# Column-tiled token values and a re-ordered second softmax half in a segment-recurrent attention kernel

## The chip, the cores and the metric

The kernel runs on one core of a Trainium2 chip. The metric is the device time of one execution in microseconds. The kernel before was run three times: 953.64, 951.12 and 949.33 us, median 951.12. The profile is one further execution.

The engines are named as in the profile: PE is TensorE (PEld its weight loads, which overlap the matmuls), DVE is VectorE, ACT is ScalarE, POOL is GpSimd, SP is SyncE, which issues DMAs here.

## The reference

A layer with two blocks on 2048 tokens of width 640: a recurrent attention over 64 segments, and a feed-forward block.

```python
def _A_ref(x, mem0, Wq, Wk, Wv, Wo, seg_len):      # seg_len 32, M 8, H 32, Dh 128
    mem = mem0
    for s in range(n_seg):                          # 64 segments, one after the other
        h = jnp.concatenate([mem, xs], axis=1)      # 8 memory rows + 32 tokens
        q = jnp.einsum('btd,dhe->bhte', h, Wq)
        k = jnp.einsum('btd,dhe->bhte', h, Wk)
        v = jnp.einsum('btd,dhe->bhte', h, Wv)
        scores = jnp.where(mask, q @ k.T * scale, -1e9)
        p = _softmax(scores, axis=-1)
        o = jnp.einsum('bhqk,bhke->bhqe', p, v)
        o = jnp.einsum('bhte,hed->btd', o, Wo)
        mem = o[:, :M, :]                           # goes into the next segment
        outs.append(o[:, M:, :])

h  = x + _A_ref(_layernorm(x), ...)
h2 = h + _B_ref(_layernorm(h), ...)                 # relu(h @ w1 + b1)**2 @ w2 + b2
```

The memory rows of one segment are the attention's output of the segment before. That makes the 64 segments a chain.

## The kernel before, in words

`step(b, sp)` handles segment `s = 4 * b + sp`. It projects q, k and v of 32 rows: the 8 memory rows and the first 24 tokens. The last 8 tokens of each segment (the "tails") don't depend on the memory; their projections and output rounds are cut into units (`tail_units`, `wo_tail_units`) that a planner (`portion`) hands out, some 8 a step. They stand in the list `fill` and are issued on PE where it would wait.

`manual_schedule` means that each engine does its instructions in the order in which the code issues them. Nothing is moved by a scheduler. The order inside one step is:

1. `run_late`: flips (DVE transposes) of tail rows that are due, then `owed.pop()()`, the `turns` of the step before (L692 to L701): two DVE transposes that bring the token weights `pkt` and `pk` into the form that the token values need (`pTt`, `pTk`), and two POOL products `pTx`.
2. Projections q0, k0, q1, k1 (L234): 5 chunks of the depth, each with 4 matmuls of 32 weight columns by 512 moving columns that lie side by side in four column groups of the array. ACT evicts, DVE flips (L258, L488), POOL spreads the memory rows' q into `qz` (L443, L445).
3. The softmax of the memory rows, in two halves of 16 heads: `scores(n)` (L498), `soft1(n)`: max on DVE (L504) and exponential on ACT (L507), `soft2(n)`: reciprocal, a product with `same` (L514) and the weighting (L518 for half 0, L521 for half 1), and the turn into a block layout `pB`: for half 0 in `soft3` (DVE transpose L529, then four copies of one 32-partition block each, L532: one on DVE, one on ACT, two on POOL), for half 1 by L521 and the transpose L524. Between these, PE does the projection of v (L234, tiles px) and the token scores (L590). ACT evicts v in two halves (L597, L611).
4. `values(0)`, `values(1)` (L540, L545): the memory rows' outputs, column-tiled. `values_out(n)` evicts them into `oT`, half 0 on ACT (L246), half 1 on DVE (L244). Ahead of and behind `values(0)` stand fill units. Between the halves PE does two rounds of the output projection (`wo_rounds`, L270), behind `values(1)` the other 14. One round is 16 heads' worth split by `head`: 4 matmuls of 320 columns. Rounds 0 to 7 need only half 0 of `oT`, rounds 8 to 15 need half 1.
5. The token softmax on DVE and ACT (L615, L648, L650, L655, L657).
6. `wo_out`: ACT and DVE fold the output (L285 to L287) and DVE transposes it into the next step's `hT` (L382), in two parts. This is the chain to the next segment. POOL weighs the tokens in between (`weigh`, L664, L666).
7. The rest of `fill`, then `token_values(s - 1)` (L423, L428): the tokens' outputs of the segment before, 32 + 8 matmuls with 32-row weights by 128 columns and 32 moving columns, four row groups side by side, into four PSUM banks. `token_out` evicts them on ACT (L434), POOL copies the tails' part (L436).

PSUM tiles `po0` and `po1` have two banks each. `hnT0` is a buffer for the feed-forward block; some tail rows are parked in it early, and the feed-forward fills it from step 59 on.

```python
        if last:
            turns()
        else:
            owed.append(turns)
```

Of the kernel before, what the change touches and what calls it, by code (L numbers as in the profile page):

```python
# [9 lines left out]
ALU = mybir.AluOpType  # L10
AX = mybir.AxisListType
F32 = mybir.dt.float32
BF16 = mybir.dt.bfloat16
# [3 lines left out]
def kernel(  # L17
# [16 lines left out]
    nc = tc.nc  # L34
# [3 lines left out]
    SEG = 32  # L38
# [203 lines left out]
    def evac(dve, out_, in_):  # L242
        if dve:
            nc.vector.tensor_copy(out=out_, in_=in_)  # L244
        else:
            nc.scalar.copy(out=out_, in_=in_)  # L246
# [169 lines left out]
    def token_values(s, v, vt4, po):  # L416

        sp = s % 4
        pTk, pTx = back.pop()
        for i in range(HG):  # L420
            for g in range(G):
                r = slice(32 * g, 32 * g + 32)
                nc.tensor.matmul(po[0][g][:, i * 32:(i + 1) * 32], lhsT=v[r, i * E:(i + 1) * E], rhs=pTk[r, i, :],  # L423
                                 start=(i == 0), stop=False, skip_group_check=True)
        for u in range(2):
            for g in range(G):
                r = slice(32 * g, 32 * g + 32)
                nc.tensor.matmul(po[0][g][:, u * 128:(u + 1) * 128].rearrange("p (j q) -> p j q", q=32)[:, :, 0:TL],  # L428
                                 lhsT=vt4[r, sp, u, :], rhs=pTx[r, u], start=False, stop=True, skip_group_check=True)

    def token_out(s, po):
        for h in range(2):
            gs = slice(2 * h, 2 * h + 2)
            nc.scalar.copy(out=oTg[:, gs, :, :, 0:SEG],  # L434
                           in_=po[1][h][:, :, 0:256].rearrange("p g (n j q) -> p g n j q", n=2, q=32))
        nc.gpsimd.tensor_copy(out=oTts[s // 4 % 2][:, :, s % 4 * TL:(s % 4 + 1) * TL], in_=oT[:, :, 0:TL])  # L436
# [7 lines left out]
            else:  # L444
                nc.gpsimd.tensor_copy(out=d, in_=src[:, :, 3, :])  # L445

    prevs, spent, owed = [], [0], []

    def end_output(s):
        pw = chn.tile([128, 512], F32, tag="ch", name="pw")  # L450
# [3 lines left out]
    def step(b, sp, v=None):  # L454
# [5 lines left out]
            v = s2.tile([128, EG], BF16, tag="v", name="v")  # L460
        if not ready:
            run_late(s, 1.6 - spent.pop())
            owed.pop()()
        if sp == 1 and b + 1 < NB:
            tails_v_in(b + 1, nc.sync)

# [26 lines left out]
        def scores(n):  # L493
            sm = chn.tile([128, 512], F32, tag="ch", name="sm")
            for j in range(4):
                for g in range(G):
                    p = n * 16 + g * 4 + j
                    nc.tensor.matmul(sm[32 * g:32 * g + 32, 0:NK], lhsT=qz[:, p, :], rhs=kT[:, p, :],  # L498
                                     start=(j == 0), stop=(j == 3), skip_group_check=True)
            sms[n] = sm  # L500

        def soft1(n):
            mx = s2.tile([128, 1], F32, tag="mx", name="mx")
            nc.vector.tensor_reduce(out=mx[:], in_=sms[n][:, 0:NK], op=ALU.max, axis=AX.X, negate=True)  # L504
            em = s2.tile([128, SEG + NK], BF16, tag="em", name="em", bufs=1)
            zm = s2.tile([128, 1], F32, tag="zm", name="zm")
            nc.scalar.activation(out=em[:, SEG:], in_=sms[n][:, 0:NK], func=ACT.Exp, bias=mx[:, 0:1], scale=1.0,  # L507
                                 accum_out=zm[:])
            ems[n], zms[n] = em, zm

        def soft2(n):
            rm = s2.tile([128, 1], F32, tag="rm", name="rm")
            nc.vector.reciprocal(out=rm[:], in_=zms[n][:])
            nc.vector.tensor_tensor(out=ems[n][:, 0:SEG].rearrange("p (j k) -> p j k", k=TL),  # L514
                                    in0=ems[n][:, 2 * SEG:].unsqueeze(1).to_broadcast([128, 4, TL]), in1=same[:], op=ALU.mult)
            if n == 0:
                pm = s1.tile([128, HG, TL], BF16, tag="pkt", name="pm")[:].rearrange("p i k -> p (i k)")
                nc.vector.tensor_scalar(out=pm, in0=ems[n][:, 0:2 * SEG], scalar1=rm[:, 0:1], scalar2=None, op0=ALU.mult)  # L518
                return pm
            pm = s1.tile([128, HG, 32], BF16, tag="pk", name="pm")[:].rearrange("p (g a) k -> p g (a k)", g=G)  # L520
            nc.vector.scalar_tensor_tensor(out=pm, in0=ems[n][:, 0:2 * SEG].unsqueeze(1).to_broadcast([128, G, 2 * SEG]),  # L521
                                           scalar=rm[:, 0:1], in1=own[:].unsqueeze(2).to_broadcast([128, G, 2 * SEG]),
                                           op0=ALU.mult, op1=ALU.mult)
            nc.vector.transpose(out=pBs[1][:], in_=pm)  # L524
            return pBs[1]

        def soft3(pm):
            pT = s1.tile([128, 2, 32], BF16, tag="pTt", name="pT")[:].rearrange("p u k -> p (u k)")
            nc.vector.transpose(out=pT, in_=pm)  # L529
            for g, copy in enumerate((nc.vector.tensor_copy, nc.scalar.copy, nc.gpsimd.tensor_copy, nc.gpsimd.tensor_copy)):  # L530
                r = slice(32 * g, 32 * g + 32)
                copy(out=pBs[0][r, g], in_=pT[r])  # L532
            return pBs[0]

        def values(n, pB, po):
            cols = po[:, 0, 0:128]
# [9 lines left out]
                                 start=False, stop=True, skip_group_check=True)  # L546

        def values_out(n, po):
            evac(n == 1, oT[:, n * 16:(n + 1) * 16, SEG:NK], po[:, 0, 0:128].rearrange("p (a m) -> p a m", m=M))

        project("q", wq, qT, 0)
        if not last and not ready:
# [46 lines left out]
            proj(wv, "half", lhs, 1, ps1, 0, 1)  # L599
        if not last:  # L600
            pm0 = soft2(0)
            scores(1)
            soft1(1)
            pT0 = soft3(pm0)
        if not ready:
            proj(wv, "half", lhs, 1, ps1, 1, 2)
        token_scores(1)
        if not ready:
            proj(wv, "half", lhs, 1, ps1, 2, DC)
        if not ready:  # L610
            nc.scalar.copy(out=v[:, 512:1024], in_=ps1[:])  # L611
        if not last:
            pT1 = soft2(1)
        def causal(skv):
# [9 lines left out]
        if last:  # L624
            run(fill, max(1, (len(fill) - 3) // 2), held, True)
            token_values(s - 1, *prevs[-2], po)
            token_out(s - 1, po)
            settle(held, True)
            run(fill, 2, held)
            settle(held, True)  # L630
            causal(skv)
        else:
            ahead = 0 if ready else (len(fill) + 1) // 2
            left = len(fill) - ahead
            run(fill, ahead // 2, held, True)
            values(0, pT0, po[1][0])
            values_out(0, po[1][0])
            run(fill, len(fill) - left, held)
            pw = chn.tile([128, 512], F32, tag="ch", name="pw")
            if not ready:  # L640
                wo_rounds(lambda p: oT[:, p, M:NK], pw, range(2))
            values(1, pT1, po[1][1])
            causal(skv)
            values_out(1, po[1][1])
            settle(held, True)
# [23 lines left out]
        if not last:  # L669
            if ready:  # L670
                for k in range(4):
                    run(fill, SEG0[k])
                    wo_rounds(lambda p: oT[:, p, M:NK], pw, [2 * k + h for h in (0, 1, 8, 9)])
            else:
                wo_rounds(lambda p: oT[:, p, M:NK], pw, range(2, 16))
            o = wo_out(pw, ((s + 1) // 4, (s + 1) % 4), weigh)
            if s > 1:
                store_main(o, s - 2)
            held = []
            run(fill, 100, held)  # L680
            if s:
                token_values(s - 1, *prevs[-2], po)
                token_out(s - 1, po)
            settle(held, True)
            for _, f in held:
                late.append((0.35, f, s + 1))
            tails_in((s + 1) // 4, (s + 1) % 4)
        else:
            weigh()
        spent.append(0.5 * min(len(mid), 2))  # L690
        run(mid, 2)
        def turns():  # L692
            pTt = s1.tile([128, 2, 32], BF16, tag="pTt", name="pTt")
            nc.vector.transpose(out=pTt[:], in_=pkt[:].rearrange("p (u j) k -> p u (j k)", u=2))
            pTx = s1.tile([128, 2, 4, TL], BF16, tag="pTx", name="pTx")
            for u in range(2):
                nc.gpsimd.tensor_tensor(out=pTx[:, u], in0=pTt[:, u, 0:TL].unsqueeze(1).to_broadcast([128, 4, TL]),
                                        in1=same[:], op=ALU.mult)
            pTk = s1.tile([128, HG, 32], BF16, tag="pTk", name="pTk")
            nc.vector.transpose(out=pTk[:], in_=pk[:])  # L700
            back.append((pTk, pTx))  # L701
        if last:
            turns()
        else:
            owed.append(turns)

    NT = 512
    NK4 = NT // 128
# [35 lines left out]
    f1T = ck(FC * NT).rearrange("p (c t) -> p c t", c=FC)  # L744
    hnT0 = const.tile([128, DC, NT], BF16, name="hnT0")
    ht0 = [const.tile([128, D], BF16, name="ht0%d" % k) for k in range(NK4)]
    halves = lambda t: [(t[:, 0:512], False), (t[:, 512:1024], False)]
    parked = halves(s2.tile([128, EG], BF16, tag="v", name="parkv"))
    parked += halves(oTts[0][:].rearrange("p h r -> p (h r)"))
# [337 lines left out]
```

## Time and profile before

| What | Value |
|---|---|
| Median of three runs | 951.12 us (949.33 to 953.64) |
| The profiled execution | 947.79 us, span 945.8 us |
| PE busy | 919.7 us (97%) |
| DVE busy | 696.5 us (74%) |
| ACT busy | 553.4 us (59%) |
| POOL busy | 311.6 us (33%) |
| One step in the middle of the loop | 11.7 to 12.2 us |
| Granted TensorE clock | 0.998 |

A line of the trace in order of time reads: start in us from the span's start, duration in us, engine, line of the kernel, operation, output tile, inputs, shapes, count, and in brackets the idle time before it and what ended it. Instructions of one kind that follow each other are merged into one row. Matmul ends are modelled, so starts are the safer numbers: the distance between the starts of two groups is what the first one cost.

A group's row in the list of waits counts a weight load's idle time in full, also where the matmuls before it were still streaming.

### The profile page before, as it was taken

Reading aid. Unit: us, or ns where it says so; the run is one execution under the profiler, and the core shown is the slowest. Engines: PE = TensorE matmul, PEld = TensorE weight load, DVE = VectorE, ACT = ScalarE, POOL = GpSimd, SP = SyncE. Lnnn points to the kernel's source line nnn. Section 1 sums busy time; section 2 is a strip of 40 time slices with the busy share of each in tenths; the row PEclk is TensorE's granted clock in tenths of the full one; section 3 lists DMA queues with packets and bytes.
Section 4 is the critical chain, followed back from the end, with each engine's and each line's share of the span. In section 5 each row is a group of like instructions: output and inputs, shape, how many; then the busy total and the mean of one; then the engine's idle time right before and its main releaser. Section 6 shows DMA issues by size and latency. Waiting matters only on the chain.

```text
span 945.8 us, 55978 instructions
## 1 busy us (share of the span) xinstructions
PE 919.7 (97%) x24749; PEld 537.0 (57%) x24760; DVE 696.5 (74%) x2131; ACT 553.4 (59%) x1460; POOL 311.6 (33%) x1002
## 2 busy tenths in 40 slices
PE   5979999999999999999999999999999999999998
PEld 2435555555555565555555656566556555565555
DVE  5168888778877887777878787878887888556632
ACT  2546666666666666666666666666666666523321
POOL 2123333333333333333333333333333333343300
PEclk9999999999999999999999999999999999999999
DMA  9983201010101000100111010101010221734320
GB/s 352 405 270 70 41 19 29 14 30 14 23 20 28 18 20 25 21 25 9 37 22 24 11 30 14 32 15 31 8 33 7 54 43 21 221 93 92 91 57 28
DMA packets 65875, 56.66 MB, mean 60 GB/s; under 512 B 37384, under 2 KB 61712, under 8 KB 63712
## 3 DMA queue, kind: packets, MB, share of 16 engines
q1 hardware_dynamic: 65392, 52.74, 20.1%
q8 instruction: 194, 3.18, 1.5%
q14 instruction: 49, 0.40, 0.2%
q0 software_dynamic: 224, 0.33, 0.1%
q10 hardware_dynamic: 16, 0.01, 0.0%
HBM read 38.37 MB, written 9.44 MB: 51 GB/s over the span
## 4 chain that ended last, share of the span: by engine, by line
PE 90%; DMA 4%; DVE 2%; SPq 2%; ACT 1%; issue 1%; POOL 0%; ACTq 0%; DVEq 0%
PE ps L234 23%; PE px L234 21%; PE pw L270 16%; PE pk L234 7%; PE y L1044 6%; PE ps L992 6%; PE ps L270 3%; DMA wq<-in_A_Wq_dram 2%; PE po L423 2%; SPq L151 2%; PE po L540 1%; PE sm L498 1%; PE ps L590 1%; DMA wo<-in_A_Wo_dram 1%; PE po L545 1%
## 5 line engine op out<-in xcount | busy, mean ns | idle before, releaser
L234 PEld LDWEIGHTS <-hT 128*32 128x32 bf16 x7680 | 182.1, 96 | 158.7 <-DVE hT L382 22.1
L270 PE MATMUL pw<-wo,oT 128*32 128x320 bf16 x4224 | 168.7, 299 | 3.5 <-DMA wo<-in_A_Wo_dram 1.2
L234 PE MATMUL px<-wv,hT 128*32 128x512 bf16 x2520 | 166.5, 377 | 0.0
L270 PEld LDWEIGHTS <-oT 128*32 128x32 bf16 x4224 | 110.4, 96 | 45.8 <-ACT oT L246 20.7
L258 DVE STREAM_TRANSPOSE qT<-row 128x512 bf16<-128x512 bf16 x128 | 89.0, 696 | 24.9 <-ACT row L253 24.3
L664 POOL TENSOR_TENSOR pkt<-ek,rk 128x64 bf16<-128x64 bf16 x64 | 18.9, 295 | 254.5 <-ACT otmp L286 248.5
L655 ACT ACTIVATE ek<-tk 128x320 bf16<-128x320 f32 x64 | 30.1, 471 | 106.1 <-DVE tk L650 106.1
L234 PE MATMUL ps<-wq,hT 128*32 128x512 bf16 x1260 | 81.5, 383 | 3.2 <-DVE hT L382 2.8
L234 PE MATMUL ps<-wk,hT 128*32 128x512 bf16 x1280 | 80.3, 379 | 0.0
L234 PE MATMUL px<-wq,hT 128*32 128x512 bf16 x1260 | 79.2, 379 | 0.0
L234 PE MATMUL pk<-wk,hT 128*32 128x512 bf16 x1240 | 78.0, 379 | 0.0
L1000 ACT ACTIVATE wv<-ps,b1f 128x512 bf16<-128x512 f32 (+1 forms) x56 | 37.6, 672 | 66.6 <-PE ps L992 66.1
L434 ACT CAST oT<-po 128x512 bf16<-128x512 f32 x128 | 68.7, 589 | 10.2 <-PE po L428 5.6
L234 PEld LDWEIGHTS <-hTt 128*32 128x32 bf16 x1920 | 53.3, 97 | 35.2 <-issue 3.3
L443 POOL COPY qz<-qT 128x96 bf16<-128x96 bf16 x126 | 33.5, 266 | 86.0 <-DVE qT L258 85.7
L1044 PE MATMUL y<-wq,wk 128*128 128x320 bf16 x416 | 58.9, 299 | 0.2
L485 ACT CAST row<-ps 128x256 bf16<-128x256 f32 x126 | 40.8, 375 | 30.0 <-PE ps L234 29.1
L253 ACT ACTIVATE row<-ps 128x512 bf16<-128x512 f32 x93 | 54.7, 611 | 5.2 <-PE ps L234 4.3
L253 ACT ACTIVATE row<-px 128x512 bf16<-128x512 f32 x63 | 37.6, 597 | 32.2 <-PE px L234 30.6
L498 PEld LDWEIGHTS <-qz 128*32 128x32 bf16 x2016 | 37.6, 95 | 25.8 <-issue 2.0
L532 POOL COPY pB<-pT 32x64 bf16<-32x64 bf16 x126 | 29.4, 233 | 66.0 <-DVE pT L529 63.4
L285 ACT COPY otmp<-pw 64x96 f32<-64x96 f32 (+2 forms) x129 | 28.9, 224 | 37.9 <-DVE o L287 20.4
(137 smaller groups left out, 1854.7 us busy)
## 6 DMA issues: line engine op xcount, KB each, us to landing
wv<-in_A_Wv_dram SPq DMA_DIRECT2D x5, 1024.0 KB
wq<-in_A_Wq_dram SPq DMA_DIRECT2D x5, 1024.0 KB
wk<-in_A_Wk_dram SPq DMA_DIRECT2D x5, 1024.0 KB
wo<-in_A_Wo_dram SPq DMA_DIRECT2D x8, 640.0 KB
o_all<-o SPq DMA_DIRECT2D x256, 7.5 KB
vt<-vt_d SPq DMA_DIRECT2D x60, 64.0 KB
xt<-in_A_x_dram SPq DMA_DIRECT2D x19, 160.0 KB
wq<-in_B_w_dram SPq DMA_DIRECT2D x1, 2080.0 KB
```

Of the source, the lines that this page charges most:

```text
L234: nc.tensor.matmul(ps[32 * k:32 * k + 32, :], lhsT=lhs(c), rhs=wr[:, c, n, k], start=(c == 0), stop=(c == DC - 1))
L253: nc.scalar.mul(out=row, in_=ps, mul=scale)
L258: nc.vector.transpose(out=dst[:, n * 16:(n + 1) * 16, 0:32], in_=row.rearrange("p (h e) -> p h e", e=32))
L270: nc.tensor.matmul(pw[32 * j:32 * j + 32, c0:c0 + DH], lhsT=lhs(p), rhs=wov2[:, head(p), ch], start=(h == 0), stop=(h == 15))
L434: nc.scalar.copy(out=oTg[:, gs, :, :, 0:SEG], in_=po[1][h][:, :, 0:256].rearrange("p g (n j q) -> p g n j q", n=2, q=32))
L443: nc.gpsimd.tensor_copy(out=d.rearrange("p a (j f) -> p a j f", j=3)[:, :, :, 0:M], in_=src[:, :, 0:3, :])
L485: nc.scalar.copy(out=row[:, u * 256:(u + 1) * 256], in_=ps[:, u * 256:(u + 1) * 256])
L498: nc.tensor.matmul(sm[32 * g:32 * g + 32, 0:NK], lhsT=qz[:, p, :], rhs=kT[:, p, :], start=(j == 0), stop=(j == 3), skip_group_check=True)
L655: nc.scalar.activation(out=ek[:], in_=tk[:], func=ACT.Exp, scale=1.0)
L992: nc.tensor.matmul(ps[:], lhsT=w1[:, c, fc * 128:(fc + 1) * 128], rhs=hnT[:, c, :], start=(c == 0), stop=(c == DC - 1))
L1000: nc.scalar.activation(out=r[:, 0:w], in_=ps[:, 0:w], func=ACT.Relu, bias=b1f[:, fc:fc + 1], scale=1.0)
L1044: nc.tensor.matmul(y[hh][:, 0:DH], lhsT=f1T[:, fc, k * 128:(k + 1) * 128], rhs=w2[:, fc, cs], start=(fc == 0 and not hf), stop=(fc == FFUL ...
```

## The change

Five things are done.

- In steps 5 to 57 (`wide`) the token values are column-tiled: the token weights are laid out as block diagonals, `pBk` (128 x 8 x 128) by four POOL copies of a 32-partition block a step, and `pBx` (128 x 2 x 128) by two POOL products, which replace the two for `pTx`. Both lie in `hnT0`. The weights of the matmul are 32 columns of all 128 rows of `v`, and 128 columns move; the outputs lie in one bank each of `po0` and `po1`. In step 5 POOL clears `pBk` and makes a mask `both`. The copies are issued by `diagonal(s - 1)` in step s, behind `soft1(1)`.
- `soft3` of the first half (its transpose and the ACT and POOL copies) is issued ahead of `scores(1)` and the second max; the DVE copy comes behind that max.
- The second half of v is evicted in two copies of 256 columns, one ahead of `values_out(0)` and one behind it. `values_out(1)` goes from DVE to ACT.
- Four output rounds instead of two stand ahead of `values(1)`.
- `turns` is no longer owed to the next step's start; its instructions are issued at the end of the step, ahead of `run_late`.

```diff
@@ token_values
         pTk, pTx = back.pop()
+        if wide(s):
+            for n in range(2):
+                for j in range(4):
+                    for k in range(4):
+                        nc.tensor.matmul(po[1][n][32 * k:32 * k + 32, 1, j * 128:(j + 1) * 128],
+                                         lhsT=v[:, (n * 4 + j) * E + 32 * k:(n * 4 + j) * E + 32 * k + 32],
+                                         rhs=pBk[:, n * 4 + j], start=(j == 0), stop=False, skip_group_check=True)
+                for k in range(4):
+                    nc.tensor.matmul(po[1][n][32 * k:32 * k + 32, 1, :].rearrange("p (a q) -> p a q", q=32)[:, :, 0:TL],
+                                     lhsT=vt4[:, sp, n, 32 * k:32 * k + 32], rhs=pBx[:, n],
+                                     start=False, stop=True, skip_group_check=True)
+            return
...
+    def wide(s):
+        return 5 <= s <= NS - 7
+
+    def diagonal(s):
+        if s == 4:
+            nc.gpsimd.memset(pBk, 0.0)
+            for g in range(G):
+                nc.gpsimd.tensor_tensor(out=both[:, :, g], in0=same[:],
+                                        in1=own[:, g:g + 1].unsqueeze(2).to_broadcast([128, 4, TL]), op=ALU.mult)
+        if wide(s):
+            pTk = back[-1][0]
+            for g in range(G):
+                r = slice(32 * g, 32 * g + 32)
+                nc.gpsimd.tensor_copy(out=pBk[r, :, 32 * g:32 * g + 32], in_=pTk[r])
+
     def token_out(s, po):
         for h in range(2):
+            if wide(s):
+                nc.scalar.copy(out=oT[:, h * 16:(h + 1) * 16, 0:SEG].rearrange("p (g j) q -> p j g q", j=4),
+                               in_=po[1][h][:, 1, :].rearrange("p (j g q) -> p j g q", j=4, g=G))
+                continue
...
         if not ready:
             run_late(s, 1.6 - spent.pop())
-            owed.pop()()
...
-        def soft1(n):
+        def soft1(n, then=None):
             mx = s2.tile([128, 1], F32, tag="mx", name="mx")
             nc.vector.tensor_reduce(out=mx[:], in_=sms[n][:, 0:NK], op=ALU.max, axis=AX.X, negate=True)
+            if then:
+                then()
...
-            for g, copy in enumerate((nc.vector.tensor_copy, nc.scalar.copy, nc.gpsimd.tensor_copy, nc.gpsimd.tensor_copy)):
+            def part(g):
                 r = slice(32 * g, 32 * g + 32)
-                copy(out=pBs[0][r, g], in_=pT[r])
-            return pBs[0]
+                (nc.vector.tensor_copy, nc.scalar.copy, nc.gpsimd.tensor_copy, nc.gpsimd.tensor_copy)[g](out=pBs[0][r, g], in_=pT[r])
+            for g in range(1, G):
+                part(g)
+            return pBs[0], lambda: part(0)
...
-            evac(n == 1, oT[:, n * 16:(n + 1) * 16, SEG:NK], po[:, 0, 0:128].rearrange("p (a m) -> p a m", m=M))
+            evac(False, oT[:, n * 16:(n + 1) * 16, SEG:NK], po[:, 0, 0:128].rearrange("p (a m) -> p a m", m=M))
...
             pm0 = soft2(0)
+            pT0, then = soft3(pm0)
             scores(1)
-            soft1(1)
-            pT0 = soft3(pm0)
+            soft1(1, then)
+        if s and not last:
+            diagonal(s - 1)
...
-            nc.scalar.copy(out=v[:, 512:1024], in_=ps1[:])
+            nc.scalar.copy(out=v[:, 512:768], in_=ps1[:, 0:256])
+            if last:
+                nc.scalar.copy(out=v[:, 768:1024], in_=ps1[:, 256:512])
...
             values_out(0, po[1][0])
+            if not ready:
+                nc.scalar.copy(out=v[:, 768:1024], in_=ps1[:, 256:512])
...
-                wo_rounds(lambda p: oT[:, p, M:NK], pw, range(2))
+                wo_rounds(lambda p: oT[:, p, M:NK], pw, range(4))
...
-                wo_rounds(lambda p: oT[:, p, M:NK], pw, range(2, 16))
+                wo_rounds(lambda p: oT[:, p, M:NK], pw, range(4, 16))
...
-        def turns():
-            pTt = s1.tile([128, 2, 32], BF16, tag="pTt", name="pTt")
...
-        if last:
-            turns()
-        else:
-            owed.append(turns)
+        pTt = s1.tile([128, 2, 32], BF16, tag="pTt", name="pTt")
+        nc.vector.transpose(out=pTt[:], in_=pkt[:].rearrange("p (u j) k -> p u (j k)", u=2))
+        pTx = s1.tile([128, 2, 4, TL], BF16, tag="pTx", name="pTx")
+        for u in range(2):
+            if wide(s):
+                nc.gpsimd.tensor_tensor(out=pBx[:, u].rearrange("p (a q) -> p a q", q=TL),
+                                        in0=pTt[:, u, 0:TL].unsqueeze(1).to_broadcast([128, 16, TL]),
+                                        in1=both[:].rearrange("p j g q -> p (j g) q"), op=ALU.mult)
+                continue
+            nc.gpsimd.tensor_tensor(out=pTx[:, u], in0=pTt[:, u, 0:TL].unsqueeze(1).to_broadcast([128, 4, TL]),
+                                    in1=same[:], op=ALU.mult)
+        pTk = s1.tile([128, HG, 32], BF16, tag="pTk", name="pTk")
+        nc.vector.transpose(out=pTk[:], in_=pk[:])
+        back.append((pTk, pTx))
...
+    hn0 = hnT0[:].rearrange("p c t -> p (c t)")
+    pBk = hn0[:, 0:1024].rearrange("p (i a) -> p i a", a=128)
+    pBx = hn0[:, 1024:1280].rearrange("p (u a) -> p u a", a=128)
+    both = hn0[:, 1280:1408].rearrange("p (j g q) -> p j g q", j=4, g=G)
```

More of the change, by code (lines that the diff above doesn't have):

```diff
@@ L445, in spread @@
                 nc.gpsimd.tensor_copy(out=d, in_=src[:, :, 3, :])
-    prevs, spent, owed = [], [0], []
+    prevs, spent = [], [0]
     def end_output(s):
@@ L691, in step @@
         run(mid, 2)
-        def turns():
-            pTt = s1.tile([128, 2, 32], BF16, tag="pTt", name="pTt")
[L694 to L701, printed above, removed]
-        if last:
-            turns()
-        else:
-            owed.append(turns)
+        pTt = s1.tile([128, 2, 32], BF16, tag="pTt", name="pTt")
[12 more added lines that the diff above has]
+        back.append((pTk, pTx))
     NT = 512
```

## The prediction

> **What bounds the kernel now.** I read the page's busy line first, then the trace in order of time, in two places: the seam between two segment steps (408 to 412 us) and the middle of a step (414 to 418 us). The page:
>
> ```profile
> PE 919.7 (97%) x24749; PEld 537.0 (57%) x24760; DVE 696.5 (74%) x2131; ACT 553.4 (59%) x1460; POOL 311.6 (33%) x1002
> ```
>
> PE is busy for 97% of the span, but its ends are modelled. So I use starts. The seam:
>
> ```profile
> 408.21 0.39 PE L234 MATMUL ps<-wv,hTt 128*32 128x512 bf16 x4
> 408.53 0.27 PEld L423 LDWEIGHTS <-v 32*128 32x128 bf16 x32 [0.42 <-issue]
> 408.53 0.37 PE L423 MATMUL po<-pTk,v 32*128 32x32 bf16 x32
> 408.59 0.28 DVE L382 STREAM_TRANSPOSE hT<-o 128x96 bf16<-128x96 bf16 x1
> 408.75 0.24 PE L428 MATMUL po<-pTx,vt 32*128 32x32 bf16 x8
> 408.92 1.30 PE L234 MATMUL ps<-wq,hT 128*32 128x512 bf16 x20
> 411.13 1.25 PE L234 MATMUL px<-wq,hT 128*32 128x512 bf16 x20
> 412.21 1.25 PE L234 MATMUL ps<-wk,hT 128*32 128x512 bf16 x20
> ```
>
> The last two rows give the price of PE work: 20 matmuls, four side by side in four column groups, so 5 rounds, fill 412.21 - 411.13 = 1.08 us. That is 0.216 us for a round of 512 columns, 0.422 ns a column, and 0.054 us for a round of 128. By this price the round begun at 408.21 is through at 408.43. The row-tiled token values (L423, weights 32x128) begin only at 408.53, 0.10 us later; the projection behind them begins at 408.92, some 0.11 us after the last L428 matmul began (by its single start, which the merged row hides). Token values thus cost 0.48 to 0.49 us: 0.10 to get in, 0.275 from first to last start, 0.11 to get out. The L382 row says what comes next: the recurrent memory's first part ends at 408.87, and PE goes on 0.05 us later. Both limits, PE's queue and the memory's chain, end within 0.01 us of each other here. Summing over single starts what PE didn't stream, steps 2 to 62 lose 32 us in all (0.5 us of 12 in a step), and 18 of these are at the token values. So no edit can win much: PE streams nearly all the time.
>
> The middle of a step:
>
> ```profile
> 414.65 0.15 DVE L514 TENSOR_TENSOR em<-em,same 128x32 bf16<-128x32 bf16 x1
> 414.84 0.24 DVE L518 TENSOR_SCALAR pm<-em,rm 128x64 bf16<-128x64 bf16 x1
> 415.14 0.20 DVE L504 TENSOR_REDUCE mx<-sm 128x1 f32<-128x40 f32 x1
> 415.26 0.23 DVE L529 STREAM_TRANSPOSE pT<-pm 128x64 bf16<-128x64 bf16 x1
> 415.44 0.29 ACT L507 ACTIVATE em<-sm,mx 128x40 bf16<-128x40 f32 x1
> 415.62 0.51 POOL L532 COPY pB<-pT 32x64 bf16<-32x64 bf16 x2 [0.96 <-DVE pT L529]
> 415.85 0.24 ACT L532 COPY pB<-pT 32x64 bf16<-32x64 bf16 x1
> 415.93 0.22 DVE L514 TENSOR_TENSOR em<-em,same 128x32 bf16<-128x32 bf16 x1
> 416.19 0.48 DVE L521 SCALAR_TENSOR_TENSOR pm<-em,rm,own 128x256 bf16<-128x256 bf16 x1
> 416.28 0.27 PE L540 MATMUL po<-pB,v 128*32 128x32 bf16 x16
> 416.67 0.27 ACT L246 CAST oT<-po 128x128 bf16<-128x128 f32 x1
> 416.71 0.45 DVE L524 STREAM_TRANSPOSE pB<-pm 128x256 bf16<-128x256 bf16 x1
> 416.99 0.46 PE L270 MATMUL pw<-wo,oT 128*32 128x320 bf16 x8
> 417.27 0.27 PE L540 MATMUL po<-pB,v 128*32 128x32 bf16 x16
> ```
>
> Here the first half's values (L540 at 416.28) wait for nothing, the output rounds (L270 at 416.99) wait for oT, and the second half's values (417.27) come when pB is just there: L524 ends at 417.16.
>
> **The change part by part.**
>
> *Column-tiled token values (53 steps).* The 40 row-tiled matmuls become 40 column-tiled ones with 128 moving columns: 10 rounds of 0.054 = 0.54 us, without the 0.10 and 0.11 at the seams. Against what the token values and the wait behind them take today, step by step: 32 of the 53 take under 0.50 us, 8 between 0.50 and 0.54, and 13 over 0.54, where the memory's chain or a stray stall ends last and the longer work is hidden. The sum of what is missing to 0.54 is +1.9 us; with no cover at all it is 53 x 0.06 = +3.2. I take +1.9.
>
> *POOL's share of it.* Each step adds four copies of 32x256 on POOL behind the first half's two. POOL's rows for 256-element copies have 0.40 to 0.42 us, so 1.6 us. They start at about 416.0 and must end before that step's token values at 420.2, so POOL itself has room; the two pBx products grow from 0.24 to at most the 0.62 of a 128x256 product each, in a stretch before the next step's spread. The cost is elsewhere. The first L514 above takes 0.15 us alone, the second 0.22 beside POOL's copy: by single starts that copy ends at 416.13 and L514 at 416.16. In most steps it is so, L514 ending 28 ns behind POOL's copy. An earlier step shows when it isn't:
>
> ```profile
> 69.32 0.54 POOL L532 COPY pB<-pT 32x64 bf16<-32x64 bf16 x2 [1.33 <-DVE pT L529]
> 69.60 0.16 DVE L514 TENSOR_TENSOR em<-em,same 128x32 bf16<-128x32 bf16 x1
> ```
>
> There POOL's second copy had begun 9 ns before L514, L514 was not delayed, and the copy took 0.27 instead of 0.23. I read this as a resource that one of the two holds while it moves data, taken some 0.13 us after POOL's recorded start and 0.10 after DVE's. In the changed kernel L521 (two SBUF operands, as L514) meets the four copies; no row of before shows that pair together, so I bound it. Times in the step above, moved by the change: the first half's transpose goes from 415.26 to 415.11 and the second max behind it to 415.26; ACT's copy comes first, 415.41 to 415.65, so the second exponential starts at 415.68 instead of 415.44, and everything behind it is 0.24 late. pB of the second half is ready at 417.16 + 0.24 = 417.40, plus 0.05 to PE. Four output rounds instead of two last from 416.99 to 416.99 + 4 x 0.136 = 417.53 (0.136 = 320 x 0.422), so PE arrives 0.08 us after pB. This slack is all there is. If L521 waits for the second copy: the first holds until 416.33 to 416.42, L514 ends 0.03 later, the second holds 0.27 more, to 416.68 to 416.76; L521 then needs its 0.37 of data, the transpose 0.48 more, PE 0.05: 417.58 to 417.66. Stall 0.05 to 0.13 a step, mean 0.085, x 53 = +4.5 us. Bounds: 0 (DVE gets there first) and 0.20 x 53 = +10.6 (rival B). I take +4.5, as most L514 rows are of the delayed kind.
>
> The Trainium skill ("SBUF — State Buffer", section "Who interferes with whom") says that a DVE instruction with two SBUF inputs contends with a GpSimd instruction that reads SBUF, and that the one issued first blocks the other for its whole instruction. By that rule the sum would hold rival B's term; the delayed L514 rows agree with it, the row at 69.60 shows that the hold starts later than the record.
>
> *First half turned ahead of the second max.* pB of the first half is ready some 0.4 us earlier. In a step like the one above nothing waited for it. Over all steps PE lost 1.9 us before L540, 0.3 in a few steps and 0.1 in several; in those with 0.3 the second half follows closer and waits in turn. I take -1.2, bounds -2.0 and 0.
>
> *Value rows in two copies, values_out(1) on ACT.* By single starts ACT's oT begins 0.22 us after the values end, takes 0.27, and PE goes on 0.05 later: 0.54 in both halves. Behind the first half two fill units cover 0.43, and the 0.11 PE loses there stays. Behind the second half 4 rounds are left, 0.54 (before: 6 rounds against 0.22 + 0.29 + 0.05 by DVE): cover and latency are equal. The second value copy (0.38, as L485's 128x256 rows) ends before 417.35, under the four rounds. Queued behind ACT's oT are a tail row's eviction and the exponential L655, which the earlier max on DVE (-0.29) lets start no later. I take 0, bounds 0 and +1.
>
> *Turns at the end of the step.* The two transposes (0.20, 0.40) run where DVE waited for a row, ahead of late flips; pTk waits for POOL's pk, 0.44 us after the memory's last transpose, and the flips queue behind. In the steps where kT was late for L498, PE lost 1.2 us in all. I take -0.4, bounds -1.2 and +1. The set-up in step 5 (a memset, four small products on POOL) hides in 4 us of idle POOL.
>
> Sum: +1.9 + 4.5 - 1.2 + 0 - 0.4 = +4.8 us. The profiled execution is 947.8 us (span 945.8 and 2.0 around it), so 952.6; it is 3.3 under the median 951.1 of the runs shown, and on that median the forecast is **955.9**. By the bounds: 1.9 - 2.0 - 1.2 = -1.3 to 3.2 + 10.6 + 1 + 1 = +15.8, or 949.8 to 966.9.
>
> **The rivals.**
>
> A, no lasting collision: L521 gets in between POOL's copies, or the slack of 0.08 covers it. For it: the 69.60 row. Sum without the 4.5: +0.3, so 951.4.
>
> B, POOL holds for the whole recorded copy (0.40 each, back to back): L521 waits until 416.85, pB at 417.69, stall 0.20, +10.6 instead of +4.5: 962. For it: the full blocking in most L514 rows; against it: 69.60.
>
> C, the faster side, decided by PE's stray stalls inside the token values: 10 of the 53 steps have a body longer than 0.275, by 1.8 us in all, in rounds that issue every 25 ns. If rounds at half that pace never starve, -1.8; if also the waits before L540 (-2.0), at kT (-1.2), and the 2.0 us lost inside the output rounds go with the calmer order, and token values add 1.9, this gives -5.1: 946. Against it: the output rounds already run at 0.136 and stall too.
>
> D, POOL is late: if a copy into the 128-wide layout takes over 1.0 us, four of them end behind the start of token values and PE waits for them; at 1.1 us each it would be 0.2 to 0.4 a step, +11 to +21: some 967. No row of POOL is near that.
>
> **How the numbers follow.** Chances: forecast 0.45, A 0.20, B 0.16, C 0.13, D 0.06. A measurement of this kernel can tell about 0.5%, 4.8 us, from no change. The forecast lies on that edge, so half of it counts as slower (0.22), 0.21 as no change, 0.02 as faster; A gives 0.13 no change and 0.07 faster; B and D are slower, C faster. Faster 0.22, same 0.34, slower 0.44. The range reaches from 945, which takes in most of C, to 966, which takes in B; the forecast's own is 950 to 962.
>
> **What would show it.** Token values one run of 40 matmuls with no idle before the weight load, 0.54 us to the next projection; L521 longer than 0.48 in most steps and PE idle before the second L540; L514's second row delayed by the copies; PE's losses before the first L540 gone. The forecast is wrong if L521 keeps 0.48 and PE doesn't wait there (A), or if PE's idle sits before the token values (D).

## The result, and the profile after

The changed kernel takes 963.48 us (median of five runs, 962.25 to 964.04), the kernel before 951.12 (five runs, 949.33 to 953.64): a ratio of 1.0138, 95% interval 1.0119 to 1.0156, some 12.4 us or 1.3% slower. The profiled execution took 962.25 us (span 960.5). The forecast was 955.9, range 945 to 966. Direction and range hold; the loss is two and a half times the +4.8 us that were forecast.

The page of the kernel after, busy line and the shares of the chain that ended last:

```profile
PE 929.4 (97%) x24749; PEld 540.7 (56%) x24760; DVE 699.7 (73%) x2068; ACT 571.3 (59%) x1586; POOL 417.4 (43%) x1219
...
PE 74%; DVE 13%; ACT 4%; DMA 4%; issue 2%; SPq 2%; POOL 0%; DVEq 0%; ACTq 0%
```

Before, the second line had PE at 90% and DVE at 2%. PE is still busy for 97% of the span, but the chain now leaves it for DVE in step after step. POOL's busy time grew by 106 us, which the chain doesn't hold at all (POOL 0%).

The seam between two steps, in order of time:

```profile
414.95 0.39 PE L234 MATMUL ps<-wv,hTt 128*32 128x512 bf16 x4
414.95 0.43 PEld L424 LDWEIGHTS <-v 128*32 128x32 bf16 x16
415.16 0.40 PE L424 MATMUL po<-hnT,v 128*32 128x128 bf16 x16
415.33 0.28 DVE L382 STREAM_TRANSPOSE hT<-o 128x96 bf16<-128x96 bf16 x1
415.39 0.23 PE L428 MATMUL po<-hnT,vt 128*32 128x128 bf16 x4
...
415.72 1.25 PE L234 MATMUL ps<-wq,hT 128*32 128x512 bf16 x20
```

The round begun at 414.95 is through at 415.17 (0.216 us a round), and the token values' first matmul is there at 415.16: no idle ahead of them and none behind. They last to the projection at 415.72, 0.55 us. This part does what was said of it.

The middle of the same kernel's step:

```profile
410.77 1.80 POOL L456 COPY hnT<-pTk 32x256 bf16<-32x256 bf16 x4
...
410.87 0.32 DVE L546 TENSOR_TENSOR em<-em,same 128x32 bf16<-128x32 bf16 x1
410.92 0.27 PE L574 MATMUL po<-pB,v 128*32 128x32 bf16 x16
...
411.23 0.65 DVE L553 SCALAR_TENSOR_TENSOR pm<-em,rm,own 128x256 bf16<-128x256 bf16 x1
411.34 0.27 ACT L246 CAST oT<-po 128x128 bf16<-128x128 f32 x1 [0.25 <-PE po L579]
411.50 0.38 ACT L677 CAST v<-px 128x256 bf16<-128x256 f32 x1
...
411.66 0.73 PE L270 MATMUL pw<-wo,oT 128*32 128x320 bf16 x16
411.91 0.45 DVE L556 STREAM_TRANSPOSE pB<-pm 128x256 bf16<-128x256 bf16 x1
...
412.47 0.20 PEld L574 LDWEIGHTS <-v 128*32 128x32 bf16 x16 [0.42 <-issue]
412.50 0.28 PE L574 MATMUL po<-pB,v 128*32 128x32 bf16 x16
```

L546, L553 and L556 are L514, L521 and L524 of before, L574 is L540, L677 half of L611. POOL's four copies start at 410.77, 0.10 us ahead of L546. The first is through at 411.16 (0.39 each), and L546 ends at 411.19: 0.32 us for what takes 0.15 alone. L553 starts beside the second copy and takes 0.65 where L521 took 0.48. So the transpose L556 ends only at 412.36. The four output rounds begun at 411.66 are through at 411.66 + 4 x 0.136 = 412.20. PE's next matmul starts at 412.50. That is 0.30 us of an idle PE: 0.16 until pB is there, and 0.14 more between pB and the matmul. Both parts come back in nearly every step. Over the single starts, PE lost 15.4 us ahead of the second half's values between 130 and 770 us of the span (54 times); before, 0.3.

That the weighting is longer in most steps, and what the row at 412.47 hides, which names no engine as releaser ("issue"), stands in the lists of each line's instructions: least, median and largest ns, then first and last start in us. First the kernel before, then the kernel after; the last two rows are the idle time ahead of L574 by releaser (us in all, times):

```profile
L521 DVE SCALAR_TENSOR_TENSOR pm<-em,rm,own x63: 483/485/486, 54.4 to 799.5; 128x256 bf16<-128x256 bf16 x63
...
L540 PEldq EVENT_SEMAPHORE  x63: 51/51/51, 54.0 to 799.0; - x63
```

```profile
L553 DVE SCALAR_TENSOR_TENSOR pm<-em,rm,own x63: 483/646/659, 54.6 to 814.4; 128x256 bf16<-128x256 bf16 x63
...
L574 PEldq EVENT_SEMAPHORE  x125: 51/51/51, 53.8 to 815.4; - x125
...
  issue: 26.5, 68
  DVE pB L556: 3.7, 18
```

The weighting's median is 646 ns where it was 485. Before, one separate wait instruction of 51 ns stood in PE's queue at the values of each step, that of the first half. After, there are two a step. The second half's first weight load waited for DVE alone before, and the matmul behind it for PE; in the changed kernel the load waits for DVE and PE, and the matmul for ACT. What ACT has to have done is the second copy of v (L677). It used to be issued ahead of the first half's `values_out`, so PE's wait for oT at the output rounds covered it. Now it stands behind that eviction on ACT, and PE has to wait for it by itself. The Trainium skill ("Perfetto Trace Analysis", section "Identifying Dependency Chains") says that an instruction which waits on several engines may have such wait instructions put in front of it; this trace shows the instruction, and what it costs is measured below.

### The profile page after: what moved, and what is told of

It reads as the page before. It is cut to its first block, busy times and chain, and to the rows that moved or that the text cites. A ratio compares the mean times of both kernels' runs of the same rounds, so it can differ in the third digit from the quotient of the medians.

```text
span 960.5 us, 56281 instructions
## 1 busy us (share of the span) xinstructions
PE 929.4 (97%) x24749; PEld 540.7 (56%) x24760; DVE 699.7 (73%) x2068; ACT 571.3 (59%) x1586; POOL 417.4 (43%) x1219
## 4 chain that ended last, share of the span: by engine, by line
PE 74%; DVE 13%; ACT 4%; DMA 4%; issue 2%; SPq 2%; POOL 0%; DVEq 0%; ACTq 0%
PE ps L234 18%; PE px L234 14%; PE pw L270 13%; PE pk L234 7%; PE y L1088 6%; PE ps L1036 6%; PE po L424 2%; DVE kT L518 2%; PE ps L270 2%; DMA wq<-in_A_Wq_dram 2%; DVE pm L553 2%; PE po L574 2%; SPq L151 2%; DVE qT L258 2%; DVE pB L556 1%
## 5 line engine op out<-in xcount | busy, mean ns | idle before, releaser
L234 PEld LDWEIGHTS <-hT 128*32 128x32 bf16 x7680 | 184.5, 96 | 157.1 <-DVE hT L382 21.5
L270 PEld LDWEIGHTS <-oT 128*32 128x32 bf16 x4224 | 103.1, 96 | 51.9 <-ACT oT L246 29.2
L456 POOL COPY hnT<-pTk 32x256 bf16<-32x256 bf16 x212 | 88.9, 419 | 9.7
L246 ACT CAST oT<-po 128x128 bf16<-128x128 f32 x126 | 33.3, 265 | 77.6 <-PE po L579 76.5
L234 PEld LDWEIGHTS <-hTt 128*32 128x32 bf16 x1920 | 50.5, 97 | 37.2 <-issue 3.0
L461 ACT CAST oT<-po 128x512 bf16<-128x512 f32 x106 | 56.9, 589 | 1.9 <-PE po L428 0.4
```

Source lines behind the costliest of these rows:

```text
L234: nc.tensor.matmul(ps[32 * k:32 * k + 32, :], lhsT=lhs(c), rhs=wr[:, c, n, k], start=(c == 0), stop=(c == DC - 1))
L270: nc.tensor.matmul(pw[32 * j:32 * j + 32, c0:c0 + DH], lhsT=lhs(p), rhs=wov2[:, head(p), ch], start=(h == 0), stop=(h == 15))
L456: nc.gpsimd.tensor_copy(out=pBk[r, :, 32 * g:32 * g + 32], in_=pTk[r])
L461: nc.scalar.copy(out=oT[:, h * 16:(h + 1) * 16, 0:SEG].rearrange("p (g j) q -> p j g q", j=4), in_=po[1][h][:, 1, :].rearrange("p (j g q) ...
```

## The experiments

Twelve kernels were run. A ratio is to the kernel before on the same chip (its medians were 949.20 us for e1 to e4, 947.88 for e5 to e8 and, on another chip, for e9 to e11, 948.35 for e12, and 951.12 for the change itself). The second table is taken from the single starts of each profiled execution: medians over some 50 steps in ns, "product" and "weighting" being the durations of the second half's two DVE instructions, "ahead" how long pB of the second half is ready before PE is free for it (negative: late), "handoff" the time from pB's end to the first matmul (where pB is early, it includes waiting for PE, and is left out).

| Run | Median us | Ratio | 95% interval |
|---|---|---|---|
| the change | 963.48 | 1.0138 | 1.0119 to 1.0156 |
| e1 copies moved | 952.00 | 1.0037 | 1.0019 to 1.0055 |
| e2 row-tiled, new order | 949.39 | 1.0000 | 0.9985 to 1.0015 |
| e3 before, with unused copies | 955.06 | 1.0053 | 1.0032 to 1.0074 |
| e4 before, with unused fills | 949.97 | 1.0008 | 0.9991 to 1.0026 |
| e5 one copy stays | 950.17 | 1.0014 | 1.0004 to 1.0024 |
| e6 six rounds ahead | 963.11 | 1.0148 | 1.0128 to 1.0168 |
| e7 old order, column-tiled | 954.23 | 1.0052 | 1.0035 to 1.0070 |
| e8 e7 with copies moved | 950.52 | 1.0021 | 1.0005 to 1.0037 |
| e9 the change, v at once | 957.22 | 1.0089 | 1.0066 to 1.0112 |
| e10 e3 with a late copy of v | 961.58 | 1.0134 | 1.0108 to 1.0159 |
| e11 e2, v at once | 946.66 | 0.9978 | 0.9964 to 0.9993 |
| e12 e1, v at once | 947.17 | 0.9990 | 0.9978 to 1.0002 |

| Kernel | product (L514, L546) | weighting (L521, L553) | ahead | handoff | PE loss a step |
|---|---|---|---|---|---|
| before | 223 | 485 | 118 | | 0 |
| after | 315 | 647 | -156 | 147 | 302 |
| e1 | 156 | 485 | 161 | | 0 |
| e3 | 224 | 665 | -57 | 54 | 111 |
| e5 | 205 | 485 | 120 | 147 | 26 |
| e6 | 315 | 647 | 118 | 147 | 28 |
| e7 | 225 | 668 | -63 | 54 | 117 |
| e9 | 319 | 649 | -161 | 55 | 216 |
| e10 | 225 | 668 | -61 | 147 | 208 |
| e12 | 155 | 485 | 156 | | 0 |

The loss is always handoff minus "ahead", within a few ns, or nothing where that is negative.

**e1, the four copies out of the softmax.** Nothing else of the change is undone.

```diff
+    def blocks_in(s, gs):
         if wide(s):
...
         tails_q_in(b, sp, 0)
+        blocks_in(s - 1, (2, 3))
...
         back.append((pTk, pTx))
+        blocks_in(s, (0, 1))
```

> The changed kernel with its four POOL copies a step moved: two directly behind the token products at the end of a step, two between the two spreads of the next, so that none runs beside the second half's softmax. Theory (POOL's copies hold up DVE's L514 and L521 counterparts, and PE waits 0.29 us in 53 steps for the second half's pB): L553 back to 0.48 us, PE's loss before the second values under 1 us instead of 15.5, time 946 to 951. Rival 1 (the 128-wide token values themselves are dear): 958 to 964. Rival 2 (the re-ordered first half alone makes the second late): PE still waits 0.1 to 0.2 a step there, 953 to 958.

Of the 13.1 us that the change costs by its ratio, 3.5 remain; the median of 952.0 lies a little above the 946 to 951 that were expected. The middle of a step, in order of time:

```profile
404.53 0.16 DVE L548 TENSOR_TENSOR em<-em,same 128x32 bf16<-128x32 bf16 x1
...
404.72 0.49 DVE L555 SCALAR_TENSOR_TENSOR pm<-em,rm,own 128x256 bf16<-128x256 bf16 x1
...
405.24 0.45 DVE L558 STREAM_TRANSPOSE pB<-pm 128x256 bf16<-128x256 bf16 x1
405.35 0.39 PEld L270 LDWEIGHTS <-oT 128*32 128x32 bf16 x16 [0.46 <-ACT oT L246]
405.35 0.73 PE L270 MATMUL pw<-wo,oT 128*32 128x320 bf16 x16
...
405.90 0.26 PE L576 MATMUL po<-pB,v 128*32 128x32 bf16 x16
```

Without the copies beside them the product takes 0.16 and the weighting 0.49, pB is there at 405.69, ahead of the rounds' end at 405.35 + 0.54 = 405.89, and PE goes on at 405.90. POOL does the same copies, 0.39 us each, elsewhere in the step: it is their place that costs.

**e2, the order edits alone.** Row-tiled token values, no copies.

```diff
     def wide(s):
-        return 5 <= s <= NS - 7
+        return False
...
```

> The changed kernel without its column-tiled token values (row-tiled in all steps, no block copies on POOL); the other four edits stay. Theory: no collision, seams of 0.10 and 0.11 us at the token values are back, the second half's pB is 0.24 later but covered by four rounds: 947 to 952, near the kernel before. Rival 2 (the order edits cost): 955 or more.

No difference. By itself the new order neither gains nor loses.

**e3 and e4, the kernel before with unused work on POOL** at the place of the copies: four copies of 32x256 out of a weight tile, and 16 fills of 32x64 that take as long (1.72 us) and read nothing.

```diff
             pT0 = soft3(pm0)
+            if 6 <= s <= NS - 6:
+                for g in range(G):
+                    r = slice(32 * g, 32 * g + 32)
+                    nc.gpsimd.tensor_copy(out=spare[r, :, 32 * g:32 * g + 32], in_=kTs[r])
...
```

> The kernel before with four POOL copies of 32x256 into an unused buffer added behind soft3, in steps 6 to 58; nothing uses them. Theory: L521 0.65 or more instead of 0.485, PE waits 0.15 to 0.25 us before the second values, 959 to 965. Rival (POOL's copies are harmless, the other edits did it): 950 to 953.

> As the last, but POOL writes zeros (16 memsets of 32x64, about as long in all) instead of copying. If POOL's reading of SBUF is what collides with DVE's second operand: L521 stays at 0.485, 950 to 953. If any POOL work there collides: L521 longer, 957 to 965.

POOL's and DVE's rows of e3 (three of the four copies lie in the stretch shown), then of e4:

```profile
407.97 1.36 POOL L608 COPY hnT<-wo 32x256 bf16<-32x256 bf16 x3
...
407.98 0.66 DVE L521 SCALAR_TENSOR_TENSOR pm<-em,rm,own 128x256 bf16<-128x256 bf16 x1
```

```profile
404.85 1.72 POOL L609 MEMSET hnT<- 32x64 bf16 x16
...
404.86 0.48 DVE L521 SCALAR_TENSOR_TENSOR pm<-em,rm,own 128x256 bf16<-128x256 bf16 x1
```

Copies hold L521 up by 0.18 us, fills not at all. So it isn't POOL's being busy, nor writes as such, but reads. The Trainium skill ("SBUF — State Buffer", section "Who interferes with whom") says just that: a DVE instruction with two SBUF inputs contends with a GpSimd instruction that reads SBUF, not with one that only writes. Both runs agree. One difference stays between the two: a fill lasts 0.11 us and a copy 0.39, and fills that last as long as a copy were not run. The size of e3 missed its expectation: +5.0 us (949.2 x 0.0053), well under what was expected. In the old order L514 is held up by the first half's two POOL copies already (224 ns, as before), so the four copies add one hold (a DVE instruction kept waiting by a POOL copy) and not two, and the handoff is 54 ns, not 147. That difference was left open until e9.

**e5, one copy stays** behind the second max, the other three are moved as in e1.

> The changed kernel with one of its four POOL copies left in place and three moved as in e1. Theory (each DVE product with two SBUF operands waits for the POOL copy under way): only L514's counterpart is held, to 0.31 us, L521's keeps 0.485; pB of the second half comes 0.16 later than in e1, which uses up the 0.16 that e1 has to spare, so PE waits 0.0 to 0.15 a step: 1 to 8 us more than e1, clearly under the changed kernel. Rival (the whole queue of copies matters, not the one under way): as e1.

A miss. The product took 205 ns, not some 310: the lone copy started earlier, 218 ns ahead of it, where the first of four starts 105 ns ahead, and so was more than half through. The ratio is below e1's rather than above, though PE loses 26 ns a step at the second values here and none in the median step of e1. What a copy costs hangs on where it falls to a tenth of a us. Why it started earlier was not followed up.

**e6, six output rounds ahead of the second values** instead of four (`range(6)` and `range(6, 16)`).

> The changed kernel with six output rounds ahead of the second values instead of four. Theory: PE's wait before the second values shrinks from 0.30 to about 0.03 a step, but two rounds (0.27) are left to cover the 0.54 from the end of the values to the next rounds, so about as much is lost inside the rounds: within 3 us of the changed kernel, the loss moved. Rival (more cover is simply better): 950 to 955.

PE's loss at the second values falls from 302 to 28 ns a step, and the time stays. By single starts PE now loses 15.0 us inside the output rounds (1.0 in the kernel after), 14 of them ahead of round 8, the first that needs the second half. pB and the values are as late as before, and so is ACT's eviction of them, which the later rounds wait for. With eight rounds waiting only for the first half, six of them ahead leave two, 0.27 us, to cover 0.54. The wait was moved, not covered.

**e7 and e8, the old order** with the column-tiled token values: e7 with the four copies in place, e8 with them moved as in e1. First half, evictions and the two rounds as before; the turns as in the change.

> The kernel before with column-tiled token values and the copies where the change puts them, but the first half's turn, the value rows, the eviction of the second values and two rounds ahead as before (the turns at the step's end as in the change). Theory: as in e3 only L521 is held (0.66), L514 keeps 0.22, PE waits about 0.11 a step: 5 to 8 us over the kernel before, less than the whole change. Rival (the copies cost the same wherever the order puts them): 11 to 15 over it.

> As e7 with the copies moved as in e1. Theory: no hold, no wait; what is left is the token values' own work, 0.55 a step against 0.49 to 0.54 with its seams: 0 to 3 us over the kernel before. Rival (128 moving columns cost more than the seams they save): 4 or more over it.

By their ratios e7 is 4.9 us over the kernel before, at the edge of what was expected, and e8 2.0, within it. The copies in place cost 3 us in the old order (1.0052 against 1.0021), where in the new order they cost 9.6 (1.0138 against 1.0037). The order edits, which e2 found neutral, triple the price of the copies. This pointed to something in the new order that only shows when pB is late, and the handoff of 147 ns, which the table has in after, e5 and e6 but in neither e3 nor e7, was the candidate.

**e9, v at once.** The kernel after, with the second half of v evicted in one copy again.

```diff
-            nc.scalar.copy(out=v[:, 512:768], in_=ps1[:, 0:256])
...
+            nc.scalar.copy(out=v[:, 512:1024], in_=ps1[:])
...
             values_out(0, po[1][0])
-            if not ready:
-                nc.scalar.copy(out=v[:, 768:1024], in_=ps1[:, 256:512])
```

> The kernel after, but the second half of the value rows is evicted in one copy ahead of the first half's values_out, as before; all else as in the change, the four copies in place. Theory: the split of that copy puts a wait for ACT at the second half's values, so their first weight load carries two waits and gets a separate wait instruction (51 ns) in PE's queue. That makes 147 ns from the end of pB to the first matmul instead of 54. With one copy the ACT wait falls away: 54 ns, PE loses 0.21 a step there instead of 0.30, 53 x 0.093 = 4.9 us less than the kernel after, ratio to before about 1.0085. Rival: the longer distance comes with the longer wait, whatever the waits are: it stays 147 ns, ratio 1.0138. Both: the weighting at 0.65 us and the product at 0.32 stay as in the kernel after.

The list of L574's instructions in e9, and the second values in order of time:

```profile
L574 PEldq EVENT_SEMAPHORE  x63: 51/51/51, 53.2 to 805.9; - x63
...
  DVE pB L556: 21.1, 56
  issue: 3.8, 14
```

```profile
408.74 0.45 DVE L556 STREAM_TRANSPOSE pB<-pm 128x256 bf16<-128x256 bf16 x1
409.24 0.17 PEld L574 LDWEIGHTS <-v 128*32 128x32 bf16 x16 [0.25 <-DVE pB L556]
409.24 0.28 PE L574 MATMUL po<-pB,v 128*32 128x32 bf16 x16
```

The second wait instruction is gone, the idle time goes to DVE's pB again, and the matmul starts 55 ns after pB. The ratio fell by 0.0049, 4.7 us; 53 steps x 0.092 are 4.9. DVE's rows are unchanged (319 and 649). The rival, that a longer wait makes a longer handoff, is out: pB is as late here as in the kernel after.

**e10, the same from the other side:** e3 with the last 16 columns of v evicted by themselves behind `values_out(0)`.

```diff
-            nc.scalar.copy(out=v[:, 512:1024], in_=ps1[:])
+            nc.scalar.copy(out=v[:, 512:1008], in_=ps1[:, 0:496])
...
             values_out(0, po[1][0])
+            if not ready:
+                nc.scalar.copy(out=v[:, 1008:1024], in_=ps1[:, 496:512])
```

> The kernel before with the four unused copies (ratio 1.0053), and the last 16 columns of the second value rows evicted in a copy of their own behind the first half's values_out. Theory of the two waits: 147 ns from the end of pB to the second half's values instead of 54, PE loses 0.20 a step there instead of 0.11, 4.9 us more than without the late copy: ratio about 1.0105. Rival: 54 ns, ratio 1.0053.

The wait instructions at the values in e10:

```profile
L540 PEldq EVENT_SEMAPHORE  x125: 51/51/51, 53.6 to 815.4; - x125
```

A copy of 16 columns suffices: two wait instructions a step, a handoff of 147, PE loss from 111 to 208 ns. The time rose by more than the 4.9 us expected, from 1.0053 to 1.0134. The first ratio that was expected, 1.0105, lies below the interval. In this execution PE also lost 6.6 us between the row-tiled token values' own starts (1.3 in e3). These are single stops in the middle of that group, up to 0.85 us long, in some 15 of the 53 steps, most of them in pairs 12 us apart that come back about every 100 us. No row shows what PE waits for there. So e10 shows the longer handoff, but its time doesn't price it.

**e11 and e12, v at once in e2 and in e1.**

> Order edits alone (token values row-tiled, no copies), with the value rows evicted at once. Theory of the two waits: pB of the second half is some 0.16 us ahead of PE here, more than 147 ns, so the split cost almost nothing: ratio 0.998 to 1.000 (1.0 with the split). Rival, the order edits gain something that the wait took back: 0.995 or lower.

> The column-tiled token values and the new order, freed of both costs: copies out of the softmax of the memory rows (ratio 1.0037 with that alone), and the value rows evicted at once. Theory: the 1.2 us that PE still lost before the second half's values go, and little else: ratio 1.001 to 1.0035. What stays over the row-tiled kernel with the same order (0.998) is then the price of the column-tiled form itself, 3 to 5 us, with the 1.1 to 2.1 us that its token values are longer and POOL's copies beside other DVE work. Rival: column-tiled values cost nothing beyond the two faults: ratio 0.998 to 0.999.

e11, the new order without split and with row-tiled token values, is the only kernel whose interval lies below 1: 0.9978, 2.1 us. By the bound of 0.5% that the prediction set this is no change, and it was run on one chip. e12 was expected at 1.001 to 1.0035 and came out at 0.9990, at the edge of the rival's range: the column-tiled token values cost nothing that can be told from e11's form once both faults are gone, and gain nothing either.

One thing does not fit. From e1 to e12, and from e2 to e11, only the split of v goes away, though the chips differ, and pB is ahead of PE in the median step of all four, so the handoff should hide. Still the time fell by 4.5 us (about ±2.1) and by 2.1 (±2.0). In the traces of e1 and e12 PE's waits ahead of the second values make up 1.2 us of the 4.5. Where the rest comes from isn't shown.

## Why the prediction was wrong in size

Three ratios split the change. Two terms were too small, that of the value rows by 4.7 us and that of the collision by 4.9. Taking the split of v away (change to e9) gives back 0.0049, 4.7 us (about ±2.8, from both intervals). Moving the copies as well (e9 to e12) gives back 0.0099, 9.4 us (about ±2.5). What remains, all else in the change, is -0.9 us (-2.1 to +0.2).

- **The step that failed: "I take 0, bounds 0 and +1"** for the value rows in two copies. It cost 4.7 us. In the traces PE's loss ahead of the second values shrinks by 53 x 0.086 = 4.6 us without it, so that place accounts for it here. The prediction asked only whether the data would be there in time, and it was: L677 ended at 411.88, half a us ahead of need. It did not ask which engines PE waits for. The copy, moved behind an eviction that PE had waited for, put one more wait on the load and matmul that stand at the critical point. The handoff became 147 ns instead of 54, which e9 takes out and e10 puts in.
- **"Stall 0.05 to 0.13 a step, mean 0.085 x 53 = +4.5", the term that was mis-sized:** right mechanism and place, half the size. Without the longer handoff the stall is 0.216 a step (e9), 11.4 us at that place and 9.4 us (±2.5) of the time, which agree. The working allowed 0.13 us of slack and moved pB by 0.13 to 0.21. The slack was 0.16 (e1), the delay 0.32: two full holds of 0.16, one on the product and one on the weighting. The first hold was mis-sized because L514's 0.22 us of before was taken as the base, while the new order had in fact freed it (0.156 in e1); the copies took that back and more. Rival B's time, 962, is near the result, but by the wrong sum: its stall of 0.20 fits the collision alone (0.216), and the split is missing from it. The range was drawn up to that rival, so that it takes the result in is luck. The 69.60 row, which spoke against it, shows a product that starts 9 ns behind POOL's copy; here the copy started 0.10 us ahead of the product in step after step, and the weighting was held though it started only some 20 ns behind a copy (5 in e3).
- **"I take +1.9" for the column-tiled token values:** their 0.54 us came out as 0.548 (median of the 53), and by single starts, over all 53 steps from the end of the work ahead to the next projection, they take 29.6 us against 28.5 before: +1.1. Together with all else it doesn't show in e12.
- **"-1.2" for the first half turned ahead:** the waits before the first values fell from 1.2 to 0.6 us between 130 and 770 us, and e2, which has this and the other order edits, with the split of v among them, measures 0.0 (±1.4 us).
- **"pB, which PE arrives 0.08 us after":** the four rounds cover the later pB, as worked out, in e1, e2, e11 and e12. They don't cover two holds.
- **Rivals A, C and D** are out: the weighting is at 0.65 in the median step, nothing gets faster, and nothing waits ahead of the token values (first matmul at the end of the stream).

## What to carry to other kernels

When work is moved on an engine, ask what every consumer waits for afterwards, not only when the data is ready: a small copy moved behind the result that another engine already waits for makes that engine wait twice, and two waits on the critical instruction cost 0.09 us here each time it is late. Put copies of POOL that read SBUF where DVE has no two-input instruction on the chain. And price edits together: here two edits that are neutral or cheap alone (new order 1.0000, column-tiled with copies 1.0052) cost 1.0138 as a pair. In the new order the copies held up two DVE instructions instead of one, and the late copy of v made each step in which pB was late dearer still.

## What the runs showed of the hardware that was not expected

- At the second values, the wait for a further engine shows only where pB is late. With two engines awaited by the load, its separate wait instruction (51 ns) is followed by the load 77 ns after that instruction's start, and the first matmul comes 147 ns after DVE's end; with one wait 54 or 55. In e1, pB is 161 ns ahead, and the longer handoff hides almost whole at that place (PE loses 1.2 us there in all).
- A held DVE instruction ends at a fixed distance behind POOL's copy: the product of 32 elements 25 to 30 ns after the copy's end (medians of e5, e9 and the kernel after), the weighting of 256 elements 0.28 us after it, over more than 40 steps. In turn the third of POOL's copies, which meets the weighting, takes 0.49 us instead of 0.39. The prediction quoted the Trainium skill ("SBUF — State Buffer", section "Who interferes with whom") for the one issued first blocking the other for its whole instruction; the section says that of DVE's 2-port modes. Here a copy that began well ahead does hold DVE, but less than its whole length is lost: 0.16 us of a 0.39 us copy, as by these times DVE starts 0.02 to 0.10 us into the copy and spends the first part of its own duration beside it. Within some 10 ns the recorded starts don't tell who holds whom: a product 9 ns behind a copy of 32x64 was not held (69.60 us, before), a weighting 5 ns behind a copy of 32x256 was (median of e3).
- The token values lost 15.1 us to PE's idle starts before and 0.4 after, in the same stretch, and the time didn't move (e12): 0.21 us of idling at the seams of each step (0.10 and 0.11) was traded for 0.24 us more from the first matmul's start to the last one's (0.513 against 0.275).
